# Splitting each expert's first layer into 256 rows and up to 512, in place of parts of up to 384

## The chip, the core and the metric

The kernel runs on one core of one Trainium2 chip. The metric is the device time of one execution in microseconds (us); a smaller number is better. TensorE (PE) multiplies matrices into PSUM, VectorE (DVE) and ScalarE (ACT) do elementwise work, GpSimd (POOL) issues the gathers and scatters, SyncE (SP) the plain loads. PEld is TensorE's weight load, which runs beside its matmuls.

## What is computed

Linear attention without a softmax, per batch and head, with an RMS norm, and on its result a mixture of 8 experts in which each token goes to one expert:

```python
kv = np.einsum('bhsd,bhse->bhde', k, v)
out = np.einsum('bhsd,bhde->bhse', q, kv)
rms = np.sqrt(np.mean(out * out, axis=-1, keepdims=True) + 1e-06)
x = (out / rms * g_norm)                      # 8 x 576 tokens of 512 columns
...
fresh_e = int(np.argmax(logits[b, s]))
if s == 0 or local_gate[b, s] < 0.5:
    e = fresh_e
else:
    e = prev_e if prev_e >= 0 else fresh_e
...
h = np.maximum(x[b, s] @ w1[e], 0.0)          # 512 -> 1024
out[b, s] = p[e] * (h @ w2[e])                # 1024 -> 512
```

Everything is fp32; p is the softmax of the token's gate logits.

## The kernel before

The first part of the program (up to about 125 us of the span) computes attention, writes each token's row to a buffer in DRAM (`xs`) and counts out which token goes where. The rest runs the experts. Expert 0's tokens come as four blocks of 128. The other seven are sorted by their number of tokens and are then called **ranks** 1 to 7; rank r has room for `WIDTHS[r - 1]` tokens, 768, 704, 640, 608, 608, 576 and 512 (L59). What is left over goes to a slow path at the end, which does not run here.

A product in fp32 is made of three matmuls on operands split into a high and a low half (`split_mm`, L1000: high by high, low by high, high by low). A rank has blocks of up to 128 tokens. For each block:

- `gather` or four times `gather4` (L801, L812): POOL fetches its rows into a tile `xr`. Rank 1 gathers whole rows, ranks 2 to 7 quarter rows, so four gathers a block. There are six `xr` buffers.
- `scale` (L1371): VectorE multiplies by the RMS factor (L842) and picks the tokens' gates (L1375 to L1381).
- `turn` (L1383): the block is transposed into its columns of the operand tiles of the first layer, `xh`/`xl` or `yh`/`yl`. In rank 1 TensorE transposes (L854), ScalarE casts the high half (L858), VectorE makes the low half (L859). In ranks 2 to 7 VectorE transposes (L831), ScalarE casts (L835), VectorE subtracts (L836).
- `second` (L1389, `products` L1019): the second layer, 24 matmuls of 512 columns (f = 0 to 7, three each), then ScalarE's scaled copy (L1039) and POOL's scatter to the output (L1040). A block of 64 tokens takes 16 matmuls (`halves`).

The first layer, `first_wide` (L1078), runs over all blocks of a **part** at once: for each f of 8 and each d of 4 three matmuls whose weights are w1 and whose moving operand is the part's tokens, 96 in all, as wide as the part. Parts of up to 256 tokens put two f into one PSUM bank. After each bank ScalarE writes the high half of h (L1074) and VectorE the low half (L1075); then come the hooks in `then`: a weight split or a block's `scale`.

`parts` (L1393) cuts a rank in two. Before, widths over 640 go into 384 and the rest, others into 256 and the rest: 384+384, 384+320, 256+384, 256+352, 256+352, 256+320, 256+256. The loop (L1433) then runs, for each rank: the first layer of part a (operand x), the second layer of its blocks (in whose hooks part b's blocks are turned into y), the first layer of part b (operand y; in its hooks the next rank's part-a blocks are scaled), the second layer of its blocks (in whose hooks those are turned into x). Gathers for the next part are dealt out as `tick`s, the weights of the next rank are split in the hooks. The order on every engine is the order of the program text (`manual_schedule`, L1430): an engine works through its own list and waits where an operand is missing.

Of the kernel before, what the change touches and what calls it, by code (L numbers as in the profile page):

```python
# [22 lines left out]
def kernel(  # L23
# [13 lines left out]
    P = 128  # L37
# [20 lines left out]

    WIDTHS = (768, 704, 640, 608, 608, 576, 512)  # L59
    NR = E - 1  # L60
    HM = 3 * P
    SPAN = 8192
    NCOL = E * KBM

# [6 lines left out]
    NF = F // P  # L71
# [85 lines left out]
    def pad(pool, nm, n=16):  # L157
        if nm not in padded:
            padded.add(nm)
            pool.tile([P, n], F32, name=nm)  # L160
# [43 lines left out]
    NW1 = ND  # L204
    NW2 = NF // 2
    to_load = []
    staged = {}
    wt = {}
# [38 lines left out]
    def wtile(pool, nm):  # L247
        if nm in ("w2_0h", "w2_4h"):
            pad(wpools[pool], "pad" + pool, 112 if pool == "s" else 48)
        t = wpools[pool].tile([P, 2 * DM], F32R, name=nm)  # L250
        if nm == "w2_0l":
            pad(wpools[pool], "past" + pool, 32)
        if nm == "w2_2l":
            pad(wpools[pool], "pad" + pool)
        return t

    def wsplit(e, i, two=False):
        t = staged.pop((e, i))

        if i < NW1:  # L260
            slot = (e * NW1 + i) % (2 * NW1)
            nm, pool = f"w1_{slot}", "s" if slot < NW1 else "b"
        else:
            slot = (e * NW2 + i - NW1) % (NW2 + 2)
            nm, pool = f"w2_{slot}", "scc"[slot] if slot < 3 else "d" if slot < NW2 else "b"
        hi, lo = (wtile(pool, nm + x) for x in "hl")
        low_ = split_w(hi, lo, t, i, e > 1)
        wt[e, i] = (hi, lo)

        def low(engine=nc.vector):  # L270
            low_(engine)
            if to_load:
                wload(*to_load.pop(0))

        if two:
            return low
        low()
# [717 lines left out]
    z = zstack.enter_context(tc.tile_pool(name="z0", bufs=1, side="right", reuse_waits="tile"))  # L995
# [16 lines left out]
    def w1s(w, d, f0, n):  # L1012
        return w[d][0][:, f0:f0 + n], w[d][1][:, f0:f0 + n]
# [64 lines left out]
    def first_wide(w, hh, hl, xh, xl, n=2 * P, then=(), each=None, late=0):  # L1078

        st = 2 if n <= 2 * P else 1  # L1080
        then = list(then)

        def pairs(f, d0, d1):
            return [(w1s(w, d, f * P, P), (xh[:, d, 0:n], xl[:, d, 0:n])) for d in range(d0, d1)]

        if late:
            phs = [ps_h.tile([P, 1, n], F32, name="ph", tag="bank") for _ in range(late)]
            for f in range(late):
                split_mm(phs[f][:, 0], pairs(f, 0, ND - 1), last=False)
                for what in then[f:f + 1]:  # L1090
                    if what:
                        what()
            for f in range(late):
                split_mm(phs[f][:, 0], pairs(f, ND - 1, ND), first=False)
                relu_split(hh[:, f:f + 1, 0:n], hl[:, f:f + 1, 0:n], phs[f], n)
        for f in range(late, NF, st):
            ph = ps_h.tile([P, st, n], F32, name="ph", tag="bank")
            for x in range(st):
                split_mm(ph[:, x], pairs(f + x, 0, ND))

            nl = n - n % P if n % P == D else n
            relu_split(hh[:, f:f + st, 0:n], hl[:, f:f + st, 0:nl], ph, nl)
            if nl < n:
                nc.vector.scalar_tensor_tensor(
                    hh[:, f:f + st, n:n + D], ph[:, :, nl:], 0.0,
                    hh[:, f:f + st, nl:n].bitcast(F32), op0=ALU.max, op1=ALU.subtract)
            if each:
                each()
            for what in then[f:f + st]:
                if what:  # L1110
                    what()
# [38 lines left out]
    def htiles(pool, n=2 * P):  # L1150
        return tuple(pool.tile([P, NF, n], F32R, name="h" + x) for x in "hl")

    def xtiles(pool, n, nm):
        return tuple(pool.tile([P, ND, n], F32R, name=nm + x, bufs=2 if nm == "t" else 1)
                     for x in "hl")

    def cidx(t, c):
        return t[:, c:c + 1]

    hh, hl = htiles(z)  # L1160
    pad(z, "padh", 40)
    w = {i: wt[0, i] for i in range(NW1)}
# [76 lines left out]
    w = {i: wt[0, i] for i in range(NW1 + NW2)}  # L1239
# [10 lines left out]
    xp = wpool("xp", "left")  # L1250
# [142 lines left out]
    def parts(r):  # L1393

        n = WIDTHS[r - 1]
        na = HM if n > 2 * HM - P else 2 * P
        bl = [Block(r, k, min(P, n - k * P), r == 1) for k in range(-(-n // P))]
        return bl[:na // P], bl[na // P:], na, n - na

# [1 line left out]

    lots = {r: parts(r) for r in range(1, E)}
    hs = htiles(z)
    xt = xtiles(xp, HM, "x")
    la, lb = lots[1][:2]
    for bl in la:
        bl.gather()
# [2 lines left out]
    turns = [lambda x=x, bl=bl: bl.turn(*xt, x * P) for x, bl in enumerate(la)]  # L1410

    i = block(z, w, fourth, gate(fourth[0], 0), cidx(sidx, 3), ps_h, ps_t, ps_y,
          {1: [split[0]], 3: [split[1]], 4: [quarters_in], 7: [split[2]], 8: [split[3]],
           **{10 + x: [bl.scale] for x, bl in enumerate(la[:2])},
           12: [turns[0], la[2].scale], 13: [turns[1]], 15: [turns[2], quarters]}, hs=hs)
    behind.append(i)
    hand.close()
    zstack.close()
    z = wpool("z")
    todo = []  # L1420

    def tick():

        if todo:
            todo.pop(0)()

    def with_ticks(hooks):
        return sorted([*hooks, *((f, tick) for f in (2, 5))], key=lambda x: x[0])

    with tc.manual_schedule(engines=order):  # L1430
        for bl in lb:
            bl.gather()
        for r in range(1, E):  # L1433
            la, lb, na, nb = lots[r]
            ma, mb_ = lots[r + 1][:2] if r + 1 < E else ([], [])
            todo = [what for bl in ma for what in bl.gathers()]
            own = [lambda j=j: wsplit(*j)
                   for j in ((r, NW1 + i) for i in range(NW2)) if j not in wt]
            nxt = [lambda i=i: wsplit(r + 1, i) for i in range(NW1 + NW2 // 2) if ma]
            hh, hl = htiles(z, HM)  # L1440

            then = [None] * NF
            for x, what in enumerate(own):
                then[x if len(own) > 2 else 2 * x] = what
            for x, bl in enumerate(lb):
                then[NF - len(lb) + x] = bl.scale
            first_wide({i: wt[r, i] for i in range(NW1)}, hh, hl, *xt, n=na, then=then, each=tick)
            w = {i: wt[r, i] for i in range(NW1 + NW2)}
            pad(xp, "padx")
            yt = xtiles(xp, HM, "y")  # L1450
            pad(xp, "pady")
            turns = [lambda x=x, bl=bl: bl.turn(*yt, x * P) for x, bl in enumerate(lb)]
            for x, bl in enumerate(la):
                hooks = []
                for f in (1, 3, 5):
                    q_ = turns if f == 3 or f == 1 and x else nxt if x else []
                    if q_:
                        hooks.append((f, q_.pop(0)))
                bl.second(w, hh, hl, x * P, with_ticks(hooks))
            while todo:  # L1460
                tick()
            while turns:
                turns.pop(0)()
            hh, hl = htiles(z, HM)
            then = [None] * NF
            for x, bl in enumerate(ma):
                then[NF - len(ma) + x] = bl.scale
            if nxt:
                then[1] = nxt.pop(0)
            if nxt:  # L1470
                then[3] = nxt.pop(0)
            if not ma:

                nc.gpsimd.drain()  # L1474
                some = read(E, NT)
            todo = [what for bl in mb_ for what in bl.gathers()]
            first_wide(w, hh, hl, *yt, n=nb, then=then, each=tick)
            xt = xtiles(xp, HM, "x")
            turns = [lambda x=x, bl=bl: bl.turn(*xt, x * P) for x, bl in enumerate(ma)]
            for x, bl in enumerate(lb):  # L1480
                left_ = len(lb) - x
                hooks = []
                for f in (1, 3, 5, 6):
                    if turns and (f in (1, 5) and left_ > 1 or left_ == 1):
                        hooks.append((f, turns.pop(0)))
                    elif nxt and f == 3:
                        hooks.append((f, nxt.pop(0)))
                end = bl.second(w, hh, hl, x * P, with_ticks(hooks), not ma and left_ == 1)
            while todo:
                tick()  # L1490
            assert not turns
            while nxt:
                nxt.pop(0)()
# [33 lines left out]
```

## Time and profile before

| | us |
|---|---|
| median of 3 runs | 561.55 (560.94 to 563.47) |
| the profiled execution | 559.78 |
| its span on the core | 557.9 |
| TensorE busy | 543.0 (97%) |
| VectorE busy | 302.8 (54%) |
| ScalarE busy | 240.5 (43%) |
| GpSimd busy | 225.6 (40%) |

An execution is 1.9 us longer than the span between its first and last instruction. Busy time of TensorE counts overlapping matmuls once; since matmuls are pipelined, the duration of one in the trace is longer than the step from one to the next, and the step is what counts. Stretches are given in us from the span's start.

### The profile page before, as it was taken

The numbers are of one execution on the slowest core, as the hardware profiler recorded it, in microseconds if no ns is written. First come the engines' busy times: TensorE is split into PE (matmuls) and PEld (weight loads), VectorE is DVE, ScalarE is ACT, GpSimd is POOL, SyncE is SP. The second block draws the span as 40 slices with busy tenths as digits, with TensorE's granted clock in tenths as the row PEclk, the third lists the DMA queues.
The fourth block names the chain that finished last, engine by engine and source line by source line (L and its number), as shares of the span: only waits on it lengthen the run. The fifth ranks groups of instructions, "written<-read, shape, count | busy, mean of one in ns | idle before, by whom it ended". The sixth has DMA issues, their size and how long they took to land. (4 is left out here: it accounts for less than half of the span.)

```text
span 557.9 us, 11774 instructions
## 1 busy us (share of the span) xinstructions
PE 543.0 (97%) x4625; PEld 478.3 (86%) x4625; DVE 302.8 (54%) x635; ACT 240.5 (43%) x440; POOL 225.6 (40%) x297
## 2 busy tenths in 40 slices
PE   8999999999899999999999999999999999999996
PEld 5787877798679899898989898989799989989894
DVE  2127876898776427355454655466455636564510
ACT  2678776851345333433433333333334333534220
POOL 4344443302257245361643673456355535531001
PEclk9999999999999999999999999999999999999999
DMA  8999999684594353332423453344334433441000
GB/s 307 361 359 361 358 344 369 227 291 179 200 321 123 128 155 115 121 112 96 152 86 109 138 157 96 115 146 145 106 134 141 118 116 133 139 118 64 19 21 31
DMA packets 38302, 95.00 MB, mean 170 GB/s; under 512 B 6229, under 2 KB 6229, under 8 KB 38238
## 3 DMA queue, kind: packets, MB, share of 16 engines
q1 hardware_dynamic: 30448, 72.73, 37.8%
q0 software_dynamic: 7744, 21.41, 12.6%
q8 instruction: 38, 0.62, 0.5%
q14 instruction: 26, 0.21, 0.1%
q10 hardware_dynamic: 46, 0.02, 0.0%
HBM read 73.92 MB, written 20.88 MB: 170 GB/s over the span
## 5 line engine op out<-in xcount | busy, mean ns | idle before, releaser
L814 POOL DMA_INDIRECT xr<-xs,gid x120 | 130.0, 1083 | 36.6 <-issue 34.8
L1075 DVE SCALAR_TENSOR_TENSOR hl<-ph,hh 128x384 fp32r<-128x384 f32 (+3 forms) x94 | 52.2, 559 | 112.4 <-ACT hh L1074 108.4
L1040 POOL DMA_INDIRECT out_dram<-ot,sidr x34 | 35.3, 1037 | 173.7 <-ACT ot L1039 128.4
L1074 ACT ACTIVATE hh<-ph 128x384 fp32r<-128x384 f32 (+4 forms) x94 | 47.0, 502 | 118.9 <-PE ph L1010 118.9
L1039 ACT ACTIVATE ot<-py,pe 128x512 f32<-128x512 f32 (+1 forms) x36 | 24.7, 687 | 60.6 <-PE py L1010 28.6
L526 DVE TENSOR_REDUCE ms<-sq 128x9 f32<-128x576 f32 x32 | 22.6, 747 | 33.2 <-POOL sq L521 32.8
L478 PE MATMUL po<-kvb,qT 128*64 128x146 f32 x512 | 39.4, 294 | 0.5 <-issue 0.5
L478 PEld LDWEIGHTS po<-kvb,qT 128*64 128x64 f32 x512 | 30.5, 136 | 5.1 <-issue 3.6
L521 POOL TENSOR_TENSOR sq<-raw 128x576 f32<-128x576 f32 x13 | 16.5, 1268 | 36.2 <-ACT raw L491 21.0
L421 POOL COPY kvb<-kvp 64x128 f32<-64x128 f32 x64 | 18.8, 294 | 22.1 <-ACT kvp L407 17.8
L842 DVE TENSOR_TENSOR xr<-xr 128x512 f32<-128x512 f32 x38 | 26.2, 690 | 2.1 <-DMA xr<-xs,gidx 2.1
L488 ACT COPY raw<-po 128x584 f32<-128x584 f32 x32 | 20.5, 640 | 13.9 <-PE po L484 11.9
L403 PEld LDWEIGHTS po<-vt,kt 64*64 64x64 f32 x1152 | 19.7, 135 | 4.6 <-issue 2.3
L835 ACT CAST yh<-xT 128x512 fp32r<-128x512 f32 x17 | 10.5, 620 | 29.8 <-DVE xT L831 29.8
L403 PE MATMUL po<-vt,kt 64*64 64x64 f32 x1152 | 22.2, 221 | 0.0
L831 DVE STREAM_TRANSPOSE xT<-xr 128x512 f32<-128x512 f32 x30 | 21.2, 706 | 0.4
L1004 PE MATMUL py<-w_1h,hh 128*128 128x512 f32 (+1 forms) x54 | 21.2, 392 | 0.0
L1010 PE MATMUL py<-w_0h,hl 128*128 128x512 f32 (+1 forms) x54 | 21.1, 391 | 0.0
L1004 PE MATMUL py<-w_0h,hh 128*128 128x512 f32 (+1 forms) x54 | 21.1, 390 | 0.0
L1009 PE MATMUL py<-w_0l,hh 128*128 128x512 f32 (+1 forms) x54 | 21.1, 390 | 0.0
L1010 PE MATMUL py<-w_1h,hl 128*128 128x512 f32 (+1 forms) x54 | 21.1, 390 | 0.0
L1009 PE MATMUL py<-w_1l,hh 128*128 128x512 f32 (+1 forms) x54 | 21.0, 390 | 0.0
(445 smaller groups left out, 1640.9 us busy)
## 6 DMA issues: line engine op xcount, KB each, us to landing
wst<-in_moe_w_dram SPq DMA_DIRECT2D x64, 512.0 KB, 3.8
xs<-raw SPq DMA_DIRECT2D x16, 584.0 KB, 6.9
kt<-in_k_dram SPq DMA_DIRECT2D x32, 288.0 KB, 4.9
vt<-in_v_dram SPq DMA_DIRECT2D x32, 288.0 KB, 5.2
qt<-in_q_dram SPq DMA_DIRECT2D x32, 288.0 KB, 4.9
xr<-xs,gid POOLq DMA_INDIRECT x120, 4.0
xs<-raw SPq DMA_DIRECT2D x4, 292.0 KB, 7.4
out_dram<-ot,sidr POOLq DMA_INDIRECT x36, 4.7
```

Of the source, the lines that this page charges most:

```text
L403: nc.tensor.matmul(pk[half(b), x, 0:D], ks[b][half(x), cd], vs[b][half(x), cd], start=(c == 0), stop=(c == C - 1))
L478: nc.tensor.matmul(out[:, :, x * HW:(x + 1) * HW], qT[:, b, w, half(x)], kvb[:, o:o + PW], start=True, stop=True)
L526: nc.vector.tensor_reduce(mss[g][:, :, 2 * n + x], sqs.pop((s, x)), axis=AX.X, op=ALU.add)
L814: i = nc.gpsimd.indirect_dma_start(out=xr[:, u * PW:(u + 1) * PW], out_offset=None, in_=xs.rearrange("t (q w) -> (t q) w", w=PW), in_offse ...
L842: (engine or nc.vector).tensor_mul(xv, xv, r.unsqueeze(3).to_broadcast([P, NP, 2, D]))
L1004: mm = nc.tensor.matmul(ps, ah, bh, start=(first and i == 0), stop=False)
L1009: nc.tensor.matmul(ps, ah, bl, start=False, stop=False)
L1010: nc.tensor.matmul(ps, al, bh, start=False, stop=(last and i == n - 1))
L1039: nc.scalar.activation(ot[0:m], po[0:m], AF.Copy, scale=pe[0:m])
L1040: return nc.gpsimd.indirect_dma_start(out=outf, out_offset=bass.IndirectOffsetOnAxis(ap=idx[0:m], axis=0), in_=ot[0:m], in_offset=None, bo ...
L1074: nc.scalar.activation(hh, ps, AF.Relu)
L1075: nc.vector.scalar_tensor_tensor(hl, ps[:, :, 0:nl], 0.0, hh[:, :, 0:nl].bitcast(F32), op0=ALU.max, op1=ALU.subtract)
```

## The change

A rank with more than 512 tokens now has a part a of 256 and a part b of all the rest (512, 448, 384, 352, 352, 320); rank 7 with its 512 has no part a, and its only part b is 512 wide. The loop learns to leave part a out: `mf` is the first part that the next rank has, `ml` its other one.

```diff
-    HM = 3 * P
+    HA, HB = 2 * P, 4 * P
...
-        na = HM if n > 2 * HM - P else 2 * P
+        na = HA if n > HB else 0
...
-    xt = xtiles(xp, HM, "x")
+    xt = xtiles(xp, HA, "x")
...
-           **{10 + x: [bl.scale] for x, bl in enumerate(la[:2])},
-           12: [turns[0], la[2].scale], 13: [turns[1]], 15: [turns[2], quarters]}, hs=hs)
+           **{10 + x: [bl.scale] for x, bl in enumerate(la)},
+           13: [turns[0]], 15: [turns[1], quarters]}, hs=hs)
...
-            todo = [what for bl in ma for what in bl.gathers()]
+            mf, ml = (ma, mb_) if ma else (mb_, [])
+            todo = [what for bl in mf for what in bl.gathers()]
...
-            hh, hl = htiles(z, HM)
+            if la:
+                hh, hl = htiles(z, HB)
+                for x, bl in enumerate(lb):
+                    then[NF - len(lb) + x] = bl.scale
+                first_wide(wf, hh, hl, *xt, n=na, then=then, each=tick)
+                w = {i: wt[r, i] for i in range(NW1 + NW2)}
+                yt = xtiles(xp, HB, "y")
+                turns = [lambda x=x, bl=bl: bl.turn(*yt, x * P) for x, bl in enumerate(lb)]
+                for x, bl in enumerate(la):
+                    hooks = []
+                    for f in (1, 3, 5):
-                    q_ = turns if f == 3 or f == 1 and x else nxt if x else []
+                        q_ = turns if f == 3 or x or len(lb) > 3 else []
+                        q_ = q_ or (nxt if x else [])
...
-            for x, bl in enumerate(ma):
-                then[NF - len(ma) + x] = bl.scale
+            for x, bl in enumerate(mf):
+                then[NF - len(mf) + x] = bl.scale
...
-            first_wide(w, hh, hl, *yt, n=nb, then=then, each=tick)
-            xt = xtiles(xp, HM, "x")
-            turns = [lambda x=x, bl=bl: bl.turn(*xt, x * P) for x, bl in enumerate(ma)]
+            first_wide(wf, hh, hl, *yt, n=nb, then=then, each=tick)
+            w = {i: wt[r, i] for i in range(NW1 + NW2)}
+            if ma:
+                xt = xtiles(xp, HA, "x")
+            elif mf:
+                yt = xtiles(xp, HB, "y")
+            to = xt if ma else yt
+            turns = [lambda x=x, bl=bl, to=to: bl.turn(*to, x * P) for x, bl in enumerate(mf)]
```

What moves, at three places. A row is a line of the kernel, an operation, out<-in and the shape; - is a row of before, + one of the kernel changed.

TensorE, in the second layer of expert 0's last block (w_2h is the weight tile of f = 4 and 5, w_3h of 6 and 7; pt<-ident,xr is a turn of a block of rank 1):

```order
+L1004 MATMUL py<-w_2h,hh 128x512
+L1009 MATMUL py<-w_2l,hh 128x512
+L1010 MATMUL py<-w_2h,hl 128x512
 L854 MATMUL pt<-ident,xr 128x128 x4
 L1004 MATMUL py<-w_2h,hh 128x512
 L1009 MATMUL py<-w_2l,hh 128x512
 L1010 MATMUL py<-w_2h,hl 128x512
+L1004 MATMUL py<-w_3h,hh 128x512
+L1009 MATMUL py<-w_3l,hh 128x512
+L1010 MATMUL py<-w_3h,hl 128x512
 L854 MATMUL pt<-ident,xr 128x128 x4
```

The first turn now stands behind the matmuls of f = 4, and two turns are left of three; the third is found in rank 1's second layer.

VectorE in rank 2, at the end of part a's first layer and the start of its second layer (xr rows are a block's `scale`, xT and yl its `turn`):

```order
+L1075 SCALAR_TENSOR_TENSOR hl<-ph,hh 128x2x256
+L842 TENSOR_TENSOR xr<-xr 128x4x128
+L1375 TENSOR_TENSOR gs<-xr,oneh 128x28
+L1379 TENSOR_TENSOR gs<-gs,oq 128x28
+L1381 TENSOR_REDUCE pe<-gs 128x1
+L842 TENSOR_TENSOR xr<-xr 128x4x128
+L1375 TENSOR_TENSOR gs<-xr,oneh 128x28
+L1379 TENSOR_TENSOR gs<-gs,oq 128x28
+L1381 TENSOR_REDUCE pe<-gs 128x1
+L831 STREAM_TRANSPOSE xT<-xr 128x4x4x32
+L836 TENSOR_TENSOR yl<-xT,yh 128x4x128
 L831 STREAM_TRANSPOSE xT<-xr 128x4x4x32
```

Two scales stand behind the last piece of h, two more ahead of it, and four turns follow where there were three.

VectorE in rank 6, in the second layer of part b (w_7l, w_4l, w_5l are low halves of rank 7's weights):

```order
+L836 TENSOR_TENSOR yl<-xT,yh 128x4x128
 L244 SCALAR_TENSOR_TENSOR w_7l<-wst,gs,w_7h 128x1024
 L831 STREAM_TRANSPOSE xT<-xr 128x4x4x32
-L836 TENSOR_TENSOR xl<-xT,xh 128x4x128
+L836 TENSOR_TENSOR yl<-xT,yh 128x4x128
+L831 STREAM_TRANSPOSE xT<-xr 128x4x4x32
+L836 TENSOR_TENSOR yl<-xT,yh 128x4x128
 L241 TENSOR_TENSOR w_4l<-wst,w_4h 128x1024
+L831 STREAM_TRANSPOSE xT<-xr 128x4x4x32
+L836 TENSOR_TENSOR yl<-xT,yh 128x4x128
 L241 TENSOR_TENSOR w_5l<-wst,w_5h 128x1024
```

Four blocks of rank 7 are turned here instead of two, into y instead of x; the split of w_4l stands ahead of the fourth turn. POOL's gathers of rank 7 keep their places; the loads on SP keep theirs throughout.

## Rows read from the trace of the kernel before

**Rows 1.** The page, busy time: engine, us (share of the span) x instructions.
```profile
PE 543.0 (97%) x4625; PEld 478.3 (86%) x4625; DVE 302.8 (54%) x635; ACT 240.5 (43%) x440; POOL 225.6 (40%) x297
```
**Rows 2.** Stretches between first and second layers: window, its length, engines' busy time (x instructions).
```profile
core 0: us, PE busy (x) PEld busy (x) DVE busy (x) ACT busy (x) POOL busy (x), PEclk, DMA share, GB/s
165.09:182.39 17.30, 17.02 (x97) 16.76 (x97) 10.99 (x20) 7.88 (x12) 12.58 (x11) 1.00 0.50 157
182.39:200.14 17.75, 17.75 (x86) 14.71 (x85) 6.10 (x10) 5.72 (x8) 4.08 (x4) 1.00 0.50 157
200.14:216.91 16.77, 16.77 (x98) 16.77 (x96) 8.15 (x16) 6.21 (x10) 10.59 (x10) 1.00 0.47 149
...
233.26:249.91 16.65, 16.65 (x98) 16.64 (x96) 8.03 (x16) 5.99 (x10) 8.63 (x9) 1.00 0.37 118
249.91:266.24 16.33, 16.33 (x74) 13.52 (x74) 8.61 (x15) 5.71 (x8) 3.03 (x3) 1.00 0.35 103
266.24:280.31 14.07, 14.07 (x98) 14.07 (x96) 6.81 (x18) 5.83 (x10) 10.12 (x10) 1.00 0.48 159
...
306.15:317.08 10.93, 10.93 (x51) 9.02 (x50) 7.47 (x16) 4.21 (x6) 7.84 (x8) 1.00 0.45 143
404.26:415.14 10.88, 10.88 (x97) 10.88 (x96) 5.65 (x9) 4.36 (x6) 5.35 (x5) 1.00 0.36 127
508.22:519.52 11.30, 11.30 (x97) 11.30 (x96) 5.20 (x6) 4.97 (x7) 0.91 (x1) 1.00 0.03 8
...
530.45:541.76 11.31, 11.31 (x98) 11.31 (x97) 2.07 (x3) 2.48 (x4) 0.98 (x1) 1.00 0.07 25
```
**Rows 3.** Timeline of PEld, expert 0's last block: start, length, [idle before it <-releaser].
```profile
161.33 0.19 PEld L1010 LDWEIGHTS py<-w_2h,hl 128*128 128x128 f32 x1 [0.16 <-DVE hl L1139]
161.93 0.42 PEld L854 LDWEIGHTS pt<-ident,xr 128*128 128x128 f32 x4 [0.41 <-DVE xr L842]
```
**Rows 4.** Timeline of DVE, rank 1, part a.
```profile
170.09 0.56 DVE L1075 SCALAR_TENSOR_TENSOR hl<-ph,hh 128x384 fp32r<-128x384 f32 x1 [3.79 <-DMA out_dram<-ot,sidx]
170.56 1.22 DVE L241 TENSOR_TENSOR w_4l<-wst,w_4h 128x1024 fp32r<-128x1024 f32 x1
171.69 0.55 DVE L1075 SCALAR_TENSOR_TENSOR hl<-ph,hh 128x384 fp32r<-128x384 f32 x1
...
183.59 0.68 DVE L842 TENSOR_TENSOR xr<-xr 128x512 f32<-128x512 f32 x1
```
**Rows 5.** Timeline of DVE, rank 3, end of part a's first layer and its second layer.
```profile
306.98 0.69 DVE L1075 SCALAR_TENSOR_TENSOR hl<-ph,hh 128x512 fp32r<-128x512 f32 x1 [1.00 <-ACT hh L1074]
307.59 0.68 DVE L842 TENSOR_TENSOR xr<-xr 128x512 f32<-128x512 f32 x1
...
308.80 0.69 DVE L842 TENSOR_TENSOR xr<-xr 128x512 f32<-128x512 f32 x1
...
309.94 0.70 DVE L831 STREAM_TRANSPOSE xT<-xr 128x512 f32<-128x512 f32 x1
...
312.06 0.71 DVE L831 STREAM_TRANSPOSE xT<-xr 128x512 f32<-128x512 f32 x1
...
315.58 0.69 DVE L836 TENSOR_TENSOR yl<-xT,yh 128x512 fp32r<-128x512 f32 x1 [0.69 <-ACT yh L835]
```
**Rows 6.** Timelines of DVE and ACT, rank 6, second layer of part b.
```profile
495.95 0.70 DVE L831 STREAM_TRANSPOSE xT<-xr 128x512 f32<-128x512 f32 x1
...
500.99 0.69 DVE L836 TENSOR_TENSOR xl<-xT,xh 128x512 fp32r<-128x512 f32 x1 [0.69 <-ACT xh L835]
...
501.44 1.04 ACT L240 CAST w_4h<-wst 128x1024 fp32r<-128x1024 f32 x1
502.52 1.23 DVE L241 TENSOR_TENSOR w_4l<-wst,w_4h 128x1024 fp32r<-128x1024 f32 x1 [0.83 <-ACT w_4h L240]
```
**Rows 7.** Timeline of POOL: the last gather of rank 7.
```profile
493.43 1.19 POOL L814 DMA_INDIRECT xr<-xs,gid  x1 [0.30 <-issue]
```
**Rows 8.** The tile xr on POOL from 493.5 to 494.5: that gather, from issue to landing.
```profile
DMA to landing us min/median/max: 3.0/3.0/3.0
```
**Rows 9.** The same from 483 to 495: the last eight gathers.
```profile
L814 POOL DMA_INDIRECT xr<-xs,gid x8: 991/998/1909, 483.4 to 493.4; - x8
...
DMA to landing us min/median/max: 2.8/3.5/5.8
```

More of the change, by code (lines that the diff above doesn't have):

```diff
@@ L1435 @@
             ma, mb_ = lots[r + 1][:2] if r + 1 < E else ([], [])
-            todo = [what for bl in ma for what in bl.gathers()]
+            mf, ml = (ma, mb_) if ma else (mb_, [])
+            todo = [what for bl in mf for what in bl.gathers()]
             own = [lambda j=j: wsplit(*j)
                    for j in ((r, NW1 + i) for i in range(NW2)) if j not in wt]
-            nxt = [lambda i=i: wsplit(r + 1, i) for i in range(NW1 + NW2 // 2) if ma]
-            hh, hl = htiles(z, HM)
+            nxt = [lambda i=i: wsplit(r + 1, i) for i in range(NW1 + NW2 // 2) if mf]
+            wf = {i: wt[r, i] for i in range(NW1)}
             then = [None] * NF
@@ L1444 @@
                 then[x if len(own) > 2 else 2 * x] = what
[L1445 to L1455, printed above, removed]
-                    q_ = turns if f == 3 or f == 1 and x else nxt if x else []
-                    if q_:
-                        hooks.append((f, q_.pop(0)))
-                bl.second(w, hh, hl, x * P, with_ticks(hooks))
@@ L1460 @@
[L1460 to L1465, printed above, removed]
-            for x, bl in enumerate(ma):
-                then[NF - len(ma) + x] = bl.scale
[L1468 to L1472, printed above, removed]
+            if la:
[11 more added lines that the diff above has]
+                        q_ = q_ or (nxt if x else [])
+                        if q_:
+                            hooks.append((f, q_.pop(0)))
+                    bl.second(w, hh, hl, x * P, with_ticks(hooks))
+                while todo:
+                    tick()
+                while turns:
+                    turns.pop(0)()
+                then = [None] * NF
@@ L1474 @@
+            hh, hl = htiles(z, HB)
+            for x, bl in enumerate(mf):
+                then[NF - len(mf) + x] = bl.scale
+            for f in (1, 3):
+                if nxt:
+                    then[f] = nxt.pop(0)
+            if not mf:
                 nc.gpsimd.drain()
                 some = read(E, NT)
-            todo = [what for bl in mb_ for what in bl.gathers()]
-            first_wide(w, hh, hl, *yt, n=nb, then=then, each=tick)
-            xt = xtiles(xp, HM, "x")
-            turns = [lambda x=x, bl=bl: bl.turn(*xt, x * P) for x, bl in enumerate(ma)]
+            todo = [what for bl in ml for what in bl.gathers()]
@@ L1487 @@
                         hooks.append((f, nxt.pop(0)))
-                end = bl.second(w, hh, hl, x * P, with_ticks(hooks), not ma and left_ == 1)
+                end = bl.second(w, hh, hl, x * P, with_ticks(hooks), not mf and left_ == 1)
             while todo:
```

## The prediction

> **What bounds the kernel now.** I read the page first: TensorE is busy 97% of the span and no other engine comes near [rows 1]. So I went to the table of stretches, cut where TensorE passes from a first layer to a second one [rows 2]. The reader is to see that its rows join without a gap: in nearly all of them TensorE's busy time is the stretch, at the full granted clock (1.00, so 2.4 GHz). From 165 us on, the time is the sum of TensorE's own matmuls. A change of the parts can help only by what one matmul costs, and hurts wherever VectorE no longer has the next operand ready in time. So the views that matter next are TensorE's and VectorE's timelines at the places where one part hands over to the next [rows 3 to 6].
>
> **What a matmul costs.** A first layer is 96 matmuls whatever its width; from the stretches [rows 2], start to start: 256 columns 11.30/96 = 117.7 ns (113.3 in another rank, 10.88/96), 320 columns 14.07/96 = 146.6, 384 columns 16.65/96 = 173.4, and 512 columns 16.33/72 = 226.8 in a second layer, which has this shape. 384 to 512 costs 53.4 ns, which is 128 columns at 2.4 GHz, so I put 448 columns, which the trace does not show, at 200.1 (halfway); its bounds are the two neighbours. A first layer of 512 columns takes 96 x 226.8 = 21.77 us. Its bound from above is 10.93/48 x 96 = 21.86, the rate behind some 256-column parts; nothing in the rows suggests less than 21.77.
>
> The Trainium skill (TensorE: Matmul & The Clock Gate, Back-to-back issue gap) gives N/2.4 + 2.5 ns for the warm gap, 215.8 ns at 512 columns and 109.2 at 256. The rows disagree with it, 226.8 and 117.7; by the page, two matmuls of 256 made into one of 512 save 2.5 ns, by the rows 2 x 117.7 - 226.8 = 8.6.
>
> **The change, part by part.** Ranks 3 to 6 keep their parts. The second layers keep their count: a block has 24 matmuls whichever part it belongs to. Tile sizes alone change there, at no cost. The weight loads keep their order on SP's queue.
>
> *Way in to rank 1.* Before, the last block of expert 0 carries three turns (four PE transposes each), now two; the third moves into rank 1's second layer, where a turn costs (17.75 - 16.33)/3 = 0.47 us [rows 2]. What goes is less than a turn: the pair of matmuls at f = 4, which now comes ahead of the first turn, has to wait for its low half of h until 161.33 either way, and the second turn then waited 0.41 for its block to be scaled [rows 3]. That wait goes, about -0.4; with +0.47 the sum is +0.05.
>
> *Rank 1.* Before 17.30 + 16.77 = 34.07; of the first, 0.65 over 16.65 is a wait for the low half of the last turn, which stays. After: 0.65 + 11.30 + 21.77 = 33.72. That is -0.35. The short part must also hold four weight splits and the first scale on VectorE before the first turn, which comes one group of three matmuls (0.68) into the second layer. VectorE's first piece of h waits there for a scatter until 170.09; from then, three pieces of h at a step of 0.6, four splits at 1.13 and one scale (0.68) end at 177.1 [rows 4, 5]. TensorE is at that turn at 165.09 - 0.4 + 0.65 + 11.30 + 0.68 = 177.3. So I take no wait. From above, each us that the scatter lands later is a us of wait; from below there is nothing to gain.
>
> *Rank 2.* 16.65 + 14.07 = 30.72 becomes 11.30 + 19.21 = 30.51: -0.21. But the second part now has four blocks, and all four must be turned by VectorE within the second layer of two blocks, 10.93 us. Rank 3 already does this with three [rows 5]: the turns start at 309.94, step by 2.12, and the last low half ends at 315.58 + 0.69 = 316.27, while TensorE gets there at 317.08 and reads the low half one matmul later, at 317.26. Slack 0.99. A fourth scale (1.21 from one to the next) falls before the last piece of h, where VectorE idled 1.00: 0.2 left over. A fourth turn adds 2.12. So 2.12 + 0.2 - 0.99 = **+1.3** of TensorE standing. From below this is 0, if the scales were ready earlier; from above 1.21 + 2.12 - 0.99 = 2.3, if that idle time doesn't cover the scale. I take 1.3, because the rows are of the same shapes. The third turn frees nothing else: ScalarE's output copy for the first block now stands behind three casts, but has a whole block of time.
>
> *Rank 7.* 11.30 + 11.31 becomes 21.77: **-0.84**; 96 matmuls fewer, the only ones removed. Its four blocks are now scaled in rank 6's second first layer and turned in its second layer. Gathers stand on POOL's queue where they stood, eight of them from 483 on; the last, issued at 493.43, landed 3.0 us later [rows 7, 8], at about 496.5. VectorE, in order, now holds its fourth scale until then, so it begins the turns at about 497.8 (496.5, and 1.2 for the scale) instead of 495.95 [rows 6]: 1.85 late. Two more turns are 4.24, and a weight split that used to follow the turns now stands ahead of the fourth: 1.23, and some 0.2 of waiting, because its cast on ScalarE (1.04) outlasts the low half ahead of it (0.69). The last turn before ended at 500.99 + 0.69 = 501.68; now 501.68 + 1.85 + 4.24 + 1.45 = 509.2. TensorE is ready at 508.22 and reads the low half 0.2 later: **+0.8**. From below 0 (the split hides under the cast it waits for); from above, the longest landing of those eight is 5.8 [rows 9], 2.8 more: 3.6.
>
> The later reading of the count and POOL's drain move from the middle of rank 7 to its start; on POOL nothing stands behind them but scatters of the last four blocks, so I cost them at nothing; uncovered, they would cost TensorE's first matmuls a fraction of a us.
>
> **Sum:** 0.05 - 0.35 - 0.21 + 1.3 - 0.84 + 0.8 = +0.75 us. The profiled execution took 559.78 us and would take 560.5; it lies 1.8 below the median of the runs shown (561.55), and the same step puts the median at 562.3. A measurement here can tell about 0.5%, 2.8 us, from no change.
>
> **The rivals.**
> *Both handovers hide.* If VectorE got ahead in ranks 2 and 6, only the matmuls count: 0.05 - 0.35 - 0.21 - 0.84 = -1.35, and with the 256-column parts of ranks 1 and 2 at 113.3 ns another -0.84: 559.4 to 560.2. For it: rank 7's margin is thin. Against it: rank 3 has less than 1 us left with three blocks. Chance 0.2. Even this is not a measurable gain.
> *The last gather is late (the slower side).* Everything rank 7 needs is behind one scale that waits for one landing. Each us that it lands later than 3.0 after its issue is a us on TensorE. Landings among those eight reach 5.8: then +0.8 becomes 3.6 and the sum +3.5, 565.1, measurably slower. It decides from a landing of about 5.1 on. For it: before, TensorE had more than 6 us of slack here (501.68 to 508.22), now none. Against it: the same gather at the same place took 3.0, and few transfers run that late. Chance 0.13.
> *Merging saves almost nothing.* If only a small fixed cost per matmul is saved, 96 of them bring 0.24 and unequal parts of the same total nothing: 0.05 + 1.3 - 0.24 + 0.8 = +1.9, 563.5. Against it: 117.7 and 226.8 in the rows. Chance 0.07. The page above gives this price.
> *The change doesn't do what it says.* TensorE's list is 96 matmuls shorter and the first layers have the new widths, so it does; chance 0.
>
> **How the numbers follow.** My forecast, no measurable change with the two handovers about equal to the savings: 0.55. The remaining 0.05 is for something I haven't seen that gains or loses matmul rate over many parts (256-column parts run at 113.3 or 117.7 without a reason I can name, 0.4 us a part). The range: from below, both handovers hidden and runs as low as those shown, 559.9; from above the late gather, 565.2. Slower takes that rival, 0.13; faster only what I haven't seen, 0.05, because all matmul savings together stay under 2.8 us; same 0.82.
>
> **What would show it.** In the profile after: stretches of about 21.8 us for rank 1's second part and rank 7's only one, and 19.2 for rank 2's; TensorE idle about 1.3 us before rank 2's second part, released by VectorE's low half, and about 0.8 before rank 7's part; in rank 6, a scale on VectorE released by the last gather. Wrong would be: no idle time at the two places (first rival), more than 3 us at rank 7 (second), 512-column first layers well off 21.8 (third), or waits in rank 1's first second layer, on a scale, which I put at nothing.

## The result and the profile after

The kernel changed took 564.92 us (median of 16 runs, 563.49 to 571.51), the kernel before 561.66 (16 runs, 560.28 to 565.09). The ratio is 1.0057, 95% interval 1.0038 to 1.0077: +3.3 us where +0.75 was forecast. The profiled execution after took 567.47 us, its span is 565.6. It lies 2.5 above its median, the one before 1.9 below its own, so the two traces differ by 7.7. Of that, 2.6 stands ahead of rank 1 (its first layer starts at 167.67 instead of 165.09), where the program is the same but for the turns in expert 0's last block. That is within what executions differ by: over the experiments on the changed kernel this start lies anywhere from 164.2 to 169.8. Each ratio is taken over the faster of two states that executions fall into; of the six runs of experiment 9 only two are in it.

The page after, busy time, with 96 matmuls fewer than [rows 1]:

```profile
PE 546.5 (97%) x4529; PEld 469.5 (83%) x4529; DVE 301.4 (53%) x627; ACT 239.6 (42%) x432; POOL 226.4 (40%) x297
```

The table of stretches after, cut at the same places as [rows 2] (columns as there):

```profile
167.67:179.29 11.62, 11.28 (x98) 11.08 (x97) 5.49 (x8) 6.26 (x8) 7.13 (x7) 1.00 0.64 214
179.29:194.25 14.96, 13.04 (x66) 10.50 (x65) 11.17 (x22) 5.84 (x8) 3.37 (x3) 1.00 0.33 117
194.25:216.03 21.78, 21.78 (x98) 18.03 (x97) 8.38 (x13) 7.08 (x10) 12.63 (x11) 1.00 0.60 178
216.03:238.15 22.12, 22.12 (x97) 18.03 (x96) 6.83 (x11) 5.69 (x8) 6.56 (x6) 1.00 0.25 85
...
249.46:261.20 11.74, 11.26 (x51) 8.82 (x49) 8.68 (x21) 3.72 (x7) 2.84 (x3) 1.00 0.27 87
261.20:281.47 20.27, 19.95 (x96) 18.14 (x97) 11.56 (x23) 8.51 (x12) 14.67 (x13) 1.00 0.57 175
281.47:301.75 20.28, 20.28 (x90) 16.51 (x88) 6.98 (x13) 5.64 (x8) 4.54 (x4) 1.00 0.24 81
...
411.18:422.50 11.32, 11.32 (x98) 11.31 (x97) 5.59 (x9) 4.35 (x6) 5.41 (x5) 1.00 0.33 114
...
501.91:516.46 14.55, 14.55 (x66) 12.02 (x65) 10.18 (x20) 6.68 (x10) 1.32 (x2) 1.00 0.19 60
516.46:538.23 21.77, 21.77 (x97) 18.02 (x96) 9.11 (x11) 7.74 (x12) 1.64 (x2) 1.00 0.05 16
538.23:560.13 21.90, 21.90 (x96) 17.83 (x95) 0.69 (x1) 2.67 (x4) 2.95 (x3) 1.00 0.11 40
```

The reader is to see three things. First layers of 512 columns take 21.77, as forecast. TensorE stands in two places where it did not before: 1.92 us in rank 1 (14.96 against 13.04), and about 0.8 around 261 in rank 2. (The 0.34 in the first row has its like, 0.28, in [rows 2].) And there is a loss without any idle time: rank 1's last second layer, 96 matmuls, takes 22.12, which is 230.4 ns each; 226.8 was counted on. Rank 5's short part takes 11.32 where it took 10.88, though nothing of rank 5 was changed.

The waits themselves, TensorE's timeline after:

```profile
182.05 0.66 PE L854 MATMUL pt<-ident,xr 128*128 128x128 f32 x4 [1.92 <-DVE xr L842]
...
261.20 0.47 PE L1004 MATMUL ph<-yh,w_0h 128*128 128x448 f32 x1 [0.48 <-ACT yh L835]
262.00 0.47 PE L1009 MATMUL ph<-yl,w_0h 128*128 128x448 f32 x1 [0.32 <-DVE yl L836]
```

VectorE's timeline after, at the same places and at rank 7's last turn:

```profile
174.97 0.69 DVE L1075 SCALAR_TENSOR_TENSOR hl<-ph,hh 128x512 fp32r<-128x512 f32 x1 [6.09 <-DMA out_dram<-ot,sidx]
...
253.41 0.70 DVE L831 STREAM_TRANSPOSE xT<-xr 128x512 f32<-128x512 f32 x1
...
261.18 0.76 DVE L836 TENSOR_TENSOR yl<-xT,yh 128x512 fp32r<-128x512 f32 x1 [0.68 <-ACT yh L835]
...
515.33 0.69 DVE L836 TENSOR_TENSOR yl<-xT,yh 128x512 fp32r<-128x512 f32 x1 [0.69 <-ACT yh L835]
```

In rank 1 VectorE's first low half waits for expert 0's last scatter, which landed 6.1 us after its issue instead of 3.5. In rank 2 the chain of four turns ends late, as forecast: the last low half ends at 261.94, and TensorE, which began the part at 261.20, goes on at 262.00. At rank 7 the last low half ends at 516.02, 0.44 before TensorE gets there (516.46). The 14.55 us ahead of that are 64 matmuls at 227.3 ns: no wait.

**By rank,** us from the start of its first layer to the end of its last second layer (rank 7: to the last matmul's start). "No scatter wait" is the seventh experiment, "repaired" the eighth:

| | before | after | no scatter wait | repaired |
|---|---|---|---|---|
| rank 1 | 68.17 | 70.48 | 68.34 | 68.36 |
| rank 2 | 61.58 | 63.60 | 63.65 | 61.64 |
| rank 3 | 55.36 | 55.21 | 55.21 | 55.21 |
| rank 4 | 54.06 | 54.22 | 54.22 | 54.02 |
| rank 5 | 53.59 | 54.42 | 54.42 | 53.55 |
| rank 6 | 50.37 | 50.86 | 50.86 | 50.37 |
| rank 7 | 44.22 | 43.67 | 43.67 | 43.35 |
| sum | 387.35 | 392.46 | 390.37 | 386.50 |

**A cause that I had not expected.** The step from one matmul to the next, f by f, falls into two levels: 226.7 ns, and some 233 ns. In the last three blocks of rank 1's last second layer f = 0 to 3 step by 232 to 235 ns, f = 5 to 7 by 226.7 (f = 4 lies between), and f = 0 to 3 take their weights from another pool than f = 4 to 7. Ranks 3 and 6, whose second layers use the latter pool alone, lost nothing there. The change also drops two pads of 64 bytes a partition (`pad(xp, "padx")` and `"pady"`, ahead of and behind `yt`), so that pool lies 128 bytes lower. The addresses that the built programs give their tiles, modulo 256:

| | h | w2, pool that stays | w2, pool behind the pads | y | w1, the two pools |
|---|---|---|---|---|---|
| before, and experiment 1 | 96 | 96 | 96 | 96 | 160, 160 |
| changed, and experiment 2 | 96 | 96 | 224 | 32 | 160, 32 |
| experiments 8 and 10 | 96 | 96 | 96 | 160 | 160, 160 |

Over both traces the second-layer matmuls whose two operands agree modulo 256 step by 227.6 ns in the mean (1296 of them), those that differ by 128 by 232.6 (250; only matmuls whose two neighbours differ by as much are counted).

### The profile page after: what moved, and what is told of

The parts are those of the page before. It is cut to its first block, busy times and chain, and to the rows that moved or that the text cites. A ratio compares the mean times of both kernels' runs of the same rounds, so it can differ in the third digit from the quotient of the medians.

```text
span 565.6 us, 11564 instructions
## 1 busy us (share of the span) xinstructions
PE 546.5 (97%) x4529; PEld 469.5 (83%) x4529; DVE 301.4 (53%) x627; ACT 239.6 (42%) x432; POOL 226.4 (40%) x297
## 5 line engine op out<-in xcount | busy, mean ns | idle before, releaser
L1075 DVE SCALAR_TENSOR_TENSOR hl<-ph,hh 128x512 fp32r<-128x512 f32 (+3 forms) x86 | 50.9, 596 | 110.8 <-ACT hh L1074 104.5
L1074 ACT ACTIVATE hh<-ph 128x512 fp32r<-128x512 f32 (+5 forms) x86 | 45.7, 534 | 116.0 <-PE ph L1010 115.9
L521 POOL TENSOR_TENSOR sq<-raw 128x576 f32<-128x576 f32 x13 | 17.7, 1363 | 36.1 <-ACT raw L491 21.9
L835 ACT CAST yh<-xT 128x512 fp32r<-128x512 f32 x20 | 12.4, 621 | 37.5 <-DVE xT L831 37.5
L421 POOL COPY kvb<-kvp 64x128 f32<-64x128 f32 x64 | 18.8, 294 | 22.8 <-ACT kvp L407 16.2
L403 PE MATMUL po<-vt,kt 64*64 64x64 f32 x1152 | 22.8, 221 | 1.0 <-DMA vt<-in_v_dram 0.9
L836 DVE TENSOR_TENSOR yl<-xT,yh 128x512 fp32r<-128x512 f32 x20 | 13.9, 697 | 13.8 <-ACT yh L835 13.8
```

The lines of the kernel that those rows point to most:

```text
L403: nc.tensor.matmul(pk[half(b), x, 0:D], ks[b][half(x), cd], vs[b][half(x), cd], start=(c == 0), stop=(c == C - 1))
L1074: nc.scalar.activation(hh, ps, AF.Relu)
L1075: nc.vector.scalar_tensor_tensor(hl, ps[:, :, 0:nl], 0.0, hh[:, :, 0:nl].bitcast(F32), op0=ALU.max, op1=ALU.subtract)
```

## The experiments

The twelve experiments form three sets of four (1 to 4, 5 to 8, 9 to 12). Each set has one chip, another for each set, and its own runs of the kernel before on it: 564.64 us in the first set, 561.94 in the second, 565.69 in the third.

**1. The two pads put back into the changed kernel.**

```diff
+                pad(xp, "padx")
                 yt = xtiles(xp, HB, "y")
+                pad(xp, "pady")
```

> The changed kernel with the two 64-byte pads of the kernel before put back around the y tiles; the order of every engine stays, only addresses move (rank weights of one of the two weight pools by 128 bytes, y by 64). Theory P (placement: a second-layer matmul is slower, about 233 ns in place of 227, where the addresses of its two operands differ by 128 within 256 bytes): rank 1's last second layer goes from 22.12 to 21.8 us, rank 7's from 21.90 to 21.6, the 256-column parts of ranks 5 and 6 from 11.31 back to 10.88, in all about -2.3 us: near 562.6 beside 564.9. Rival C (the second layers are slow because of other traffic beside them): the stretches stay at 230 ns a matmul and the time at 564.9. The waits in ranks 1 and 2 stay by either.

The stretches went as the placement theory says (rank 1's last second layer, rank 5's short part):

```profile
216.78:238.56 21.78, 21.78 (x97) 18.02 (x96) 6.84 (x11) 5.69 (x8) 6.57 (x6) 1.00 0.25 87
411.39:422.28 10.89, 10.89 (x98) 10.88 (x96) 5.65 (x9) 4.36 (x6) 4.28 (x4) 1.00 0.34 117
501.52:517.92 16.40, 14.70 (x66) 11.84 (x64) 9.96 (x20) 5.56 (x9) 3.23 (x3) 1.00 0.20 63
517.92:522.17 4.25, 4.02 (x9) 2.95 (x10) 2.49 (x3) 2.78 (x4) 1.00 (x1) 0.60 0.16 62
522.17:542.47 20.30, 20.30 (x89) 16.27 (x87) 7.29 (x9) 6.06 (x9) 0.91 (x1) 1.00 0.02 4
```

The time did not: 575.12, ratio 1.0179 (1.0129 to 1.0229); no plain run of the changed kernel stands beside it in this set. The last three rows show the largest loss, 4.6 us more than the same stretches took in the trace after (40.95 against 36.32). At rank 7's start TensorE stood 1.7 us, and then ran for 4.25 us at a granted clock of 0.60, the lower level (1.2 GHz) in most of them. VectorE's timeline there, the scales of rank 7's third and fourth block:

```profile
502.47 0.69 DVE L842 TENSOR_TENSOR xr<-xr 128x512 f32<-128x512 f32 x1 [1.31 <-DMA xr<-xs,gid]
...
506.06 0.69 DVE L842 TENSOR_TENSOR xr<-xr 128x512 f32<-128x512 f32 x1 [1.90 <-DMA xr<-xs,gid]
```

TensorE's timeline, the first matmuls of rank 7:

```profile
517.92 0.50 PE L1004 MATMUL ph<-yh,w_4h 128*128 128x512 f32 x1 [1.71 <-ACT yh L835]
...
519.62 0.63 PE L1004 MATMUL ph<-yh,w_5h 128*128 128x512 f32 x1
520.04 0.63 PE L1009 MATMUL ph<-yl,w_5h 128*128 128x512 f32 x1
```

The last two scales wait for their gathers, and all turns stand behind them, as in the prediction's second rival. But what made it late was its issue more than its landing. POOL's timeline, the scatter ahead of those gathers and the last of them, first here, then in the trace after:

```profile
490.66 1.03 POOL L1040 DMA_INDIRECT out_dram<-ot,sidr  x1 [3.08 <-ACT hh L1074]
...
502.64 1.39 POOL L814 DMA_INDIRECT xr<-xs,gid  x1 [0.30 <-issue]
```

```profile
489.05 1.03 POOL L1040 DMA_INDIRECT out_dram<-ot,sidr  x1 [1.77 <-ACT ot L1039]
...
500.35 1.07 POOL L814 DMA_INDIRECT xr<-xs,gid  x1 [0.30 <-issue]
```

Rank 6's second first layer starts at 487.45 here and at 487.83 in the trace after, so the last gather was issued 15.2 us behind it instead of 12.5; its scale began 3.4 us after the issue, 3.1 in the trace after. The step of 427 ns in place of 227 to 233 is a price that I had not seen. (512-column first layers ran at 233.3 here, with y and w1 64 apart.)

**2. The two pads taken out of the kernel before.** Every engine's order stays.

> The kernel before with its two 64-byte pads taken out, nothing else. Theory P: second-layer matmuls with weights of the shifted pool go from 227 to about 233 ns, the 256-column parts of ranks 5 and 6 from 10.88 to 11.3 us: about +2.3 us, 564.0 beside 561.7. Rival C: no stretch changes, 561.7.

Measured 568.04 against 564.64, ratio 1.0054 (1.0019 to 1.0088): about +3, as placement demands and the rival excludes. How much of the 3 is placement is known from the stretches alone: in its profiled execution another 3 us went into single late steps of TensorE in ranks 2, 4, 5 and 6, for most of which it names no cause, and the kernel before has no trace on this chip to compare. Rank 2's first second layer and rank 5's short part, in [rows 2] 16.33 and 10.88:

```profile
254.75:271.32 16.57, 16.57 (x73) 13.52 (x73) 8.61 (x15) 5.71 (x8) 5.68 (x6) 1.00 0.38 116
...
411.91:423.22 11.31, 11.31 (x98) 11.31 (x96) 5.59 (x9) 4.35 (x6) 3.63 (x4) 1.00 0.37 125
```

**3 and 12. The scatter's wait.** In expert 0's pool, `h` is laid out ahead of `ot`, so that rank 1's `hl` no longer lies on the tile that the last scatter reads.

```diff
     pad(z, "padh", 40)
+    z.tile([P, F], F32, name="h", bufs=1)
```

> The changed kernel with the tile h of expert 0 laid out ahead of the two output tiles ot, so that the new low half hl of rank 1 no longer lies on the tile that the last scatter of expert 0 reads. Theory S (the wait in rank 1's first second layer, 1.92 us of TensorE, comes from that scatter, which landed 6.1 us after its issue where before 3.5, and is usual): VectorE's first piece of h in rank 1 comes within 1 us of ScalarE's, the wait on the scale goes, the stretch from 14.96 to about 13.0 us, the time about -1.9: 563.0 beside 564.9. Rival N (the late landing belongs to the profiled execution alone; 3.5 is usual): the wait goes from the profile, the time stays within 0.5 of 564.9.

> The changed kernel with h ahead of ot in expert 0's pool. In six looks at the unmended layout the wait at rank 1's first turn was 1.9, 1.4, 0.4, 0, 0 and 0 us; without the overlap it is 0 in each: about -0.6 us in the mean (not to be told from none by this many runs), and VectorE's first low half of h right behind ScalarE's high half, in this and any look. Rival: another wait takes its place (weight casts on ScalarE), and the wait at the turn stays above 0.5.

In the first of them VectorE's first low half comes 0.63 after the start of ScalarE's high half, about the duration of that, and the scatter releases nothing any more (timelines of ScalarE and VectorE):

```profile
170.65 0.60 ACT L1074 ACTIVATE hh<-ph 128x512 fp32r<-128x512 f32 x1 [3.05 <-PE ph L1010]
171.28 0.69 DVE L1075 SCALAR_TENSOR_TENSOR hl<-ph,hh 128x512 fp32r<-128x512 f32 x1 [3.23 <-issue]
```

But 0.50 of waiting was left at the first turn, behind stops of ScalarE and TensorE that the profile ascribes to nothing. In the second (12) the low half again comes 0.63 behind the high half, and the wait is gone. The times, 1.0217 (1.0161 to 1.0273) and 1.0147 (1.0087 to 1.0207), were made on the two chips where rank 7 starts late (below, 5 and 9), and tell nothing of 0.6 us. In the unmended layout the wait was 1.92 in the trace after, 1.19 in experiment 5, 0.28, 0.90, 0.68 and 1.20 in experiments 4, 9, 10 and 11, and none in 1, 6 and 7. That the scatter causes it is shown by its row in the trace after and by the same row in 5, 10 and 11; its share of the median stays open, between 0 and 2 us.

**4 and 11. Rank 2's last two scales inside its first two turns,** where VectorE waits for ScalarE's cast.

```diff
         nc.scalar.copy(hi, xT)
+        if mid:
+            mid()
         nc.vector.tensor_sub(xl[:, :, t0:t0 + P], xT, hi.bitcast(F32))
```

> The changed kernel with the scales of rank 2's third and fourth block moved from behind the last piece of h into the first two turns, where VectorE waits 0.69 us for ScalarE's cast. Theory H (TensorE's 0.81 + 0.60 us of waiting before rank 2's second part is VectorE's chain of scales and turns): the chain ends 2 x 0.69 = 1.4 us sooner, both waits fall to about 0.1, the time about -1.3: 563.6 beside 564.9. Rival G (gathers land late, so the scales can't begin sooner): the waits stay.

> The changed kernel with rank 2's last two scales inside its first two turns, as once before where the engines' stalls ahead of the place spoiled the reading. Theory H: the two waits before rank 2's second part (0.65 + 0.60 us of TensorE) go, -1.3 to -1.5 us in that rank's stretches, 564.0 where the base is 565.4. Rival: they stay.

The first of the two (1.0141, 1.0101 to 1.0181) was spoiled: VectorE's chain from the last piece of h to the last low half took 9.8 us instead of 11.5, but that piece came 3.9 us later after the start of the second layer than in the trace after, and the waits stayed. The second, in its stretches:

```profile
249.54:260.62 11.08, 11.08 (x50) 9.01 (x49) 9.36 (x23) 4.34 (x7) 5.14 (x5) 1.00 0.34 118
260.62:280.22 19.60, 19.60 (x97) 17.95 (x96) 10.85 (x23) 7.89 (x12) 15.34 (x13) 1.00 0.54 171
```

11.08 and 19.60 against 11.74 and 20.27: both waits are gone, -1.33. The time, 1.0150 (1.0097 to 1.0203), cannot be told from that set's base (experiment 9).

**5 and 9. The changed kernel again.**

> The changed kernel itself, once more, as the base of the next three on the same chip. If chips differ only by a constant, about +3.3 us on the kernel before, as measured first. Theory L (the changed kernel leans more on late landings: rank 1's short part on the last scatter of expert 0, rank 7's only part on its last gather): where transfers land later the distance to the kernel before grows, to +8 or more, and the profile shows TensorE waiting about 1.9 us at rank 7's start, as three of the first four runs did, in place of 0. The matmul steps of all second layers repeat to 0.1 ns per stretch by the placement theory.

> The changed kernel a third time, as the base for the next three on one chip. +3.0 to +3.5 us on the kernel before; stretches of the ranks as in the last two looks but for rank 1's first second layer, where the wait for expert 0's last scatter is anything from 0 to 1.9 us.

565.33 against 561.94 in the second set, ratio 1.0061 (1.0031 to 1.0091), so the first measurement repeats; so do the steps (230.5 ns over rank 1's last second layer in both traces). In the third set the six runs took 567.5 to 586.0 us; the ratio is 1.0127 (1.0026 to 1.0228), an interval that holds 1.0061 too, so these times do not show that the distance differs between chips.

The traces do show a difference. In all seven profiled executions of the changed kernel and its variants in the first and third set TensorE stood at rank 7's start, for 1.35 to 2.63 us; in the trace after and in experiment 5 it did not. In each of the seven the last gather of rank 7 was issued 15.2 us after the start of rank 6's second first layer (16.9 in experiment 11), in the trace after and in experiments 5 and 7 12.5. The scale began 3.0 to 3.7 us after that issue, against 3.1 in the trace after. So theory L is right that the kernel hangs on this gather, and in the main wrong that its landing is what is late: 2.7 us lie in the issue, at most 0.8 in the landing (2.9 in the trace after; those of the seven are not recorded, but a scale can't begin before its gather has landed). POOL had stood 3.1 to 3.7 us ahead of the scatter in front of the gathers, 1.8 in the trace after. For that the profile names the scatter before it in experiments 4 and 11 and a write of h by ScalarE in the other five; what held it is not settled.

**6. Rank 7 back in two parts** (`na = HA` for every rank).

> The changed kernel with rank 7 back in two parts of 256, nothing else. TensorE has 96 matmuls more, 22.6 us of first layers against 21.8. By my prediction the wait at rank 7's start (0 to 1.9 us in the runs so far, and up to 2.8 more where the wait lets the clock fall) is gone with the merged part. So +0.8 us on the changed kernel where that shows no wait; -1 to -4 where it does. Rival: the wait at rank 7's start stays, because it comes from the gathers and not from the count of blocks; then +0.8 in either case.

566.44, 1.1 more than the changed kernel in the same set, which showed no wait there. The intervals of the two overlap (1.0045 to 1.0100 and 1.0031 to 1.0091), so it is the stretches that show it: the merged part saves what was counted for it, 21.77 against 22.8 of first layers (11.31 and 11.51).

**7. Rank 7's third and fourth scale inside the second and third turn.**

> The changed kernel with the scales of rank 7's third and fourth block moved into the second and third turn, so that no turn stands behind the scale that waits for the last gather. Theory L7 (TensorE's wait at rank 7's start is VectorE's chain held by that gather): the chain begins some 1.5 to 3 us sooner and takes 2 x 0.5 longer, the wait is 0 also with late gathers; 0 where the changed kernel shows no wait, -2 to -4.6 us where it shows 1.9 (the second figure with the fall of the clock). Rival: the wait comes from TensorE or ScalarE (casts of weights); then no change.

565.31 beside 565.33: no change, as forecast for a chip without the wait. With late gathers it was not run.

**8. All repairs together,** with 128 bytes of padding ahead of y.

> All repairs together: 128 bytes of padding ahead of y (weights, h and y then agree modulo 256 bytes), the tile h ahead of ot, rank 2's and rank 7's scales inside the turns. If placement, the scatter and the two handovers are the whole cost, second layers run at 227 ns throughout, 512-column first layers at 226.8, no wait above 0.5 us in ranks 1, 2 and 7, and the time is that of the kernel before less what the matmuls save: -0.6 to -1.4 us (the prediction's first rival); against the changed kernel -4 or more. If something unseen costs time, it stays above the kernel before.

561.13 against 561.94, ratio 0.9974 (0.9945 to 1.0003); against the changed kernel of the same set -4.2 us. The stretches of rank 1 (last), rank 2, rank 5 and rank 7:

```profile
211.59:233.36 21.77, 21.77 (x98) 18.02 (x96) 6.83 (x11) 5.70 (x8) 6.58 (x6) 1.00 0.26 87
244.67:255.59 10.92, 10.92 (x50) 9.01 (x49) 9.09 (x21) 4.61 (x7) 3.71 (x4) 1.00 0.34 121
255.59:275.04 19.45, 19.45 (x97) 18.03 (x96) 10.77 (x22) 7.63 (x12) 13.94 (x13) 1.00 0.56 170
...
404.23:415.11 10.88, 10.88 (x97) 10.88 (x96) 5.64 (x9) 4.36 (x6) 5.15 (x5) 1.00 0.36 124
...
508.15:529.95 21.80, 21.80 (x97) 18.02 (x96) 9.11 (x11) 7.64 (x12) 1.53 (x2) 1.00 0.05 16
529.95:551.50 21.55, 21.55 (x96) 17.83 (x95) 0.69 (x1) 2.67 (x4) 2.94 (x3) 1.00 0.11 41
```

Against experiment 7 the table has 3.9 us less: 2.0 in rank 2, where the handover goes too, the rest in ranks 4 to 7, where only addresses moved. Its ranks take 386.50 where the kernel before takes 387.35. So by the stretches the new parts are worth about 1 us once nothing is lost beside them; in the times the interval just touches no change.

**10. Placement alone,** the 128 bytes ahead of y.

> The changed kernel with 128 bytes of padding ahead of y, order unchanged: placement alone. Theory P, by the stretches of the run with all repairs against the run with rank 7's alone: second layer of rank 1's last part -0.35 us, rank 2's -0.32 and its 448-column part -0.23, rank 4 -0.20, rank 5 -0.87, rank 6 -0.49, rank 7 -0.32: -2.8 us, so within 1 us of the kernel before. The rival (the first try at this showed +1.8% in time while its stretches had gone as theory P says: the time there was spent elsewhere) would leave it at +3.3.

571.46 against 565.69, ratio 1.0098 (1.0061 to 1.0135): a miss by some 5 us. The stretches did go (rank 1's last second layer 21.78, rank 5's short part 10.88). TensorE at rank 2's second part shows the largest loss:

```profile
263.84 0.47 PE L1004 MATMUL ph<-yh,w_0h 128*128 128x448 f32 x1 [3.35 <-ACT yh L835]
...
265.56 0.58 PE L1010 MATMUL ph<-yh,w_1l 128*128 128x448 f32 x1
265.93 0.58 PE L1004 MATMUL ph<-yh,w_2h 128*128 128x448 f32 x1
```

It stood 3.35 us and then fell to the lower clock (373 ns a step at 448 columns): the two stretches took 38.55 us together, 32.01 in the trace after. Rank 7 lost another 3.7 at its start, as in experiment 1. Ahead of rank 2's wait, ScalarE's third piece of h had come late:

```profile
249.50 0.60 ACT L1074 ACTIVATE hh<-ph 128x512 fp32r<-128x512 f32 x1 [5.82 <-remote]
```

What held it, the profile does not name. The padding is not what brings it: on the same chip without it, rank 2's first second layer took 14.21 and 15.81 us in experiments 9 and 12 (16.51 here, 11.74 in the trace after). In experiment 11, on that chip with the scales inside the turns, it came in time, so how much of the 3.35 that repair would take is not shown. Against its own set's base the run can't be judged (experiment 9). So no run shows the time come back by placement alone: that is shown in stretches (1, 8 and 10), and in time the other way round (2) and together with the other repairs (8).

## Why the prediction was right or wrong, point by point

The time fell inside the range, near its upper end, and on the forecast's side; the size was 2.5 us off, and the interval lies across the 0.5% that I had called the limit of a measurement. That it fell inside was luck: the upper end was there for a late gather in rank 7, and what filled it was a loss of matmul rate over many parts, for which the prediction had kept a chance of 0.05 and no us.

- **What bounds the kernel** held: TensorE 97% busy, and each gain or loss is one of matmul steps or of a late operand.
- **512-column first layers**: 21.77 forecast, 21.77 measured. The third rival (merging saves almost nothing) falls with it, as rank 7's two short parts ran at 117.7 ns before; at the 113.3 of ranks 5 and 6 it would have held (2 x 113.3 = 226.6, an estimate from those rows). The price that it drew on (the Trainium skill, TensorE: Matmul & The Clock Gate, Back-to-back issue gap: N/2.4 + 2.5 ns) is one that the page gives for a matmul by itself; no trace here shows it, 226.8 instead of 215.8 at 512 columns.
- **Way in to rank 1**: +0.05 was -0.4 in expert 0's last block and +0.47 for the turn that moves into rank 1. The block took 8.38 instead of 8.58, -0.2.
- **Rank 1**: with that turn, -0.35 + 0.47 = +0.12 was forecast for its stretches, and the table has +0.2 without the scatter's wait. Two things that I had not counted cancel in it: its last second layer at 230 ns is +0.35, its short part at 113.3 ns instead of 117.7 is -0.42. The condition that I had set ("each us that the scatter lands later is a us of wait") came true in some executions, +1.9 in the profiled one.
- **Rank 2's handover**: +1.3 forecast, and 1.33 went when the chain on which the forecast rested was shortened (experiment 11). The rank as a whole lost 2.0, not 1.1: 448 columns took 203.9 ns, not 200.1 (+0.4), and its second layers ran at 230 to 231 (+0.5).
- **Rank 7**: -0.84 for the matmuls was exact. The handover's +0.8 was nothing: the last gather was issued 12.5 us after rank 6's second first layer began, not 13.8. Those 1.3 us off the forecast's own sum leave the chain 0.5 early, and it ended 0.44 early: the chain was right, its start was not. The second layer behind it lost 0.3 to its addresses.
- **The step that failed** is "Ranks 3 to 6 keep their parts ... Tile sizes alone change there, at no cost". Those ranks lost 1.3 us (the table): 0.43 each in the short parts of ranks 5 and 6, the rest mostly in second layers. Ranks 1, 2 and 7 lost about as much again. I had counted instructions and left out where their operands lie; the change drops two pads, which the diff shown under The change leaves out. Putting them back brought 21.78 for 22.12 in rank 1's last second layer and 10.89 for 11.32 in rank 5's short part, and taking them out of the kernel before did the reverse (experiments 1 and 2).
- **The late gather** (second rival) was not what happened in the trace after. On the chips of the first and third set TensorE did stand where the rival says, but behind a gather that was issued 2.7 us late, not one that took long to land (experiments 5 and 9). In four of the seven cases it is dearer than I priced it: a stretch at the lower clock follows, and rank 7's first layer took 23.98 to 24.02 us in experiments 4, 10 and 11 against 22.40 to 22.43 in 3, 9 and 12.

The account: +0.2, +2.0 and -0.55 for ranks 1, 2 and 7, +1.3 for ranks 3 to 6 make +3.0 without the scatter's wait; with -0.2 for the way in and an open share of that wait, this agrees with the measured +3.3 (+2.1 to +4.3).

## What to carry to other kernels

A change of tile sizes is also a change of addresses: compare the addresses of a matmul's two operands before and after, and try a pad before blaming the schedule. Where a chain of another engine ends within a microsecond of TensorE's need, one trace doesn't give its cost: the same chain ended 0.44 us early in one and left TensorE standing for 1.35 to 2.63 us on two other chips, at times with a stretch at the lower clock behind it. Work that hangs on a transfer is worth moving into the idle time of such a chain: in rank 2 that took both waits away (experiment 11); in rank 7 it was not run where the gather is late.

## What the runs showed of the hardware that was not expected

- Second-layer matmuls (512 columns) step by 227.6 ns in the mean when the addresses of moving and stationary operand agree modulo 256 bytes, by 232.6 when they differ by 128 (both traces). First layers of 512 columns: 226.8 when they agree (the trace after), 233.3 at 64 apart (experiment 1). It is no rule for every width: 352 columns took 158.4 at 128 apart (rank 4, the trace after) and 160.0 where they agree (rank 4, experiment 8). The Trainium skill (SBUF — State Buffer, SBUF: two separate sides) says that TensorE never waits on anyone at SBUF's engine ports; the traces name no one that these matmuls wait for, and the cause of the difference was not tried further.
- First layers of 256 columns take 113.3 or 117.7 ns, a whole part at one level. One program gave both: rank 1's short part ran at 113.4 in the trace after and at 117.7 in experiment 5. In ranks 5 and 6 the level goes with the pads (113.3 before and in experiments 1, 8 and 10, 117.8 in the trace after and the other nine), yet rank 6's own operands keep their addresses throughout (x at 224, w1 at 160). What chooses is open.
- The length of a wait doesn't tell whether the lower clock follows. At rank 7's start it followed waits of 1.35, 1.71, 1.71 and 2.63 us (experiments 10, 1, 4 and 11: granted clock 0.60 to 0.69 over the next 4 to 5 us), and not waits of 1.70, 1.90 and 1.98 us (experiments 3, 12 and 9: 1.00).
